# First loads of a fused attention and feed-forward kernel: x0 in two column halves on two DMA queues, V weights in two contraction halves, x1 between them, x1 statistics in quarters

## Chip, cores, metric

One core of one Trainium2 chip. The metric is the device time of one execution in microseconds, median of several runs. A profiled execution also gives a span, about 1.7 us shorter than its time.

## The reference, cut to what matters

```python
# S = 2048 rows, D = 1024, 32 heads of 32, window 256, F = 3584, all bf16
h  = x + attention(layernorm(x) @ wqkv) @ wo        # causal, sliding window of 256
h2 = h + silu(layernorm(h) @ w1) @ w2
# layernorm: (x - mean) / sqrt(var + 1e-5), over the 1024 columns of a row
```

The change concerns only the first 10 us: the layer norm of the first two tiles of 128 rows (x0, x1), their transposes, and the first product with the V part of `wqkv`.

## The kernel before

The first loads, in the order in which they are issued (`queue` is SyncE's unless named):

```python
def load_x(b, j, queue=nc.sync):
    queue.dma_start(out=x_ring[(b % 2) * 4 + j], in_=x2d[(b * 4 + j) * P:(b * 4 + j + 1) * P, :])

nc.scalar.activation(out=dummy[:], in_=eps[:], func=ACT.Sqrt)   # loads ScalarE's table
load_x(0, 0)                  # x0, 256 KB
load_wqkv(2 * D)              # first V weights, 8 contraction tiles, 1 MB
load_x(0, 1, nc.scalar)       # x1, on ScalarE's queue
load_x(0, 2)
load_wqkv(2 * D + 512)        # second V weights
load_x(0, 3)
load_wqkv(0)
# cut: identity, constants
for i in range(11):           # warm-up of TensorE's clock
    nc.tensor.matmul(o_ps[i % 2][:]..., lhsT=warm[:, 0, 0:P], rhs=warm[:, 0, :], start=True, stop=True)
```

Layer norm of x0 and x1, in the order of VectorE's instructions:

```python
def ln_half(xt, stats, c):
    nc.vector.bn_stats(out=stats[:, c, :], in_=xt[:, c * 512:(c + 1) * 512])

def ln_first(xt, st, rs, j, half_done=None, ahead=None):
    ln_stats(xt, st, j, half_done)                 # one or two ln_half, then bn_aggr
    nc.scalar.activation(out=rs[:, j:j + 1], in_=st[:, j, 1:2], func=ACT.Sqrt, bias=eps[:], scale=1.0)
    if ahead is not None:
        ln_half(ahead[0], ahead[1], 0)             # x1's first half while ScalarE takes the root
    nc.vector.reciprocal(out=rs[:, j:j + 1], in_=rs[:, j:j + 1])
    for h in range(4):
        ln_norm(xt[:, h * 256:(h + 1) * 256], st, rs, j)   # in place, a quarter at a time

ln_first(x_ring[0], st, rs, 0, None, (x_ring[1], half))
turn_first(x_ring[0], lnT_b[0], 0)     # 8 transposes on TensorE, 4 copies on ScalarE
ln_first(x_ring[1], st, rs, 1, half)
v_group(0, 0, 0, act, turn_1)          # 7 matmuls of x0, transposes of x1, eighth matmul
ln_first(x_ring[2], st, rs, 2)
v_group(0, 1, 0, act)                  # from here on TensorE has work without a break
```

The softmax here doesn't subtract the row's maximum and nothing guards it: scores larger than these inputs give would overflow.

## Time and profile before

| | before |
|---|---|
| median of the first 3 runs | 697.09 us (696.58 to 697.35) |
| span of the profiled execution | 695.5 us (its time 697.29) |
| TensorE busy | 99% of the span |
| TensorE's clock granted at full | from 5.30 us on |
| x0 landed / first statistic starts | 4.31 / 4.33 us |
| x1's normalization starts | 9.05 us |
| dense stretch (17 matmuls in a row) starts | 10.34 us |

A timeline line has the start, the time from the first to the last of the merged instructions, engine, line of the program, operation, output and inputs, how many, and in brackets how long the engine had been idle and for what. The last row is the one to keep in view. After it TensorE does not rest until the end, so a shift there should be a shift of the whole time.

### The profile page before, as it was taken

To read this page: it belongs to the slowest core of one execution; us is meant where nothing else is said; L and a number is where in the kernel's file an instruction comes from. 1 tells how busy PE (TensorE), PEld (TensorE's weight loads), DVE (VectorE), ACT (ScalarE), POOL (GpSimd) and SP (SyncE) were. 2 spreads that over 40 slices of the span, in tenths; PEclk is the share of its full clock that TensorE was granted. 3 is DMA by queue.
4 is the path that set the end of the run, shared out by engine and by line. 5 is a ranking of instruction groups with operands and counts; after the bars stand their busy time and mean duration, and the time that the engine had idled before them with its cause. 6 is when DMAs were issued, how large, how long until landed. Compare 5 with 4: busy or idle time off the path is not lost.

```text
span 695.5 us, 12334 instructions
## 1 busy us (share of the span) xinstructions
PE 690.1 (99%) x5091; PEld 331.6 (48%) x5091; DVE 289.5 (42%) x616; ACT 257.9 (37%) x328; POOL 174.5 (25%) x391
## 2 busy tenths in 40 slices
PE   8999999999999999999999999999999999999998
PEld 3444444555555555544444444444444444444445
DVE  6267646644443448544316134433133251244111
ACT  4326657777777777621310023300033100233000
POOL 1007667777777777500000000000000000000000
PEclk9999999999999999999999999999999999999999
DMA  7732131026231778880123410024200023100110
GB/s 241 257 53 77 35 93 51 17 60 193 70 124 23 205 251 272 199 311 31 31 76 99 107 38 1 1 83 77 83 1 1 11 95 91 45 1 1 30 39 24
DMA packets 76457, 60.84 MB, mean 87 GB/s; under 512 B 50288, under 2 KB 60528, under 8 KB 76400
## 3 DMA queue, kind: packets, MB, share of 16 engines
q1 hardware_dynamic: 76256, 59.78, 29.9%
q8 instruction: 40, 0.66, 0.4%
q10 hardware_dynamic: 144, 0.26, 0.1%
q14 instruction: 17, 0.14, 0.1%
HBM read 39.85 MB, written 8.39 MB: 69 GB/s over the span
## 4 chain that ended last, share of the span: by engine, by line
PE 99%; DMA 1%; DVE 0%; issue 0%
PE hacc L563 19%; PE hacc L600 17%; PE acc L248 16%; PE acc L600 10%; PE acc L563 9%; PE acc L238 8%; PE acc L267 7%; PE o_ps L339 4%; PE sc L285 3%; PE hacc L267 1%; PE o_ps L354 1%; PE sc L313 1%; DMA r_o<-in_A_x_dram 1%; PE tp L216 0%; DVE ln_st L169 0%; DVE r_o L197 0%
## 5 line engine op out<-in xcount | busy, mean ns | idle before, releaser
L330 POOL TENSOR_SCALAR_AFFINE_SELECT r_e<-r_e 128x256 bf16<-128x256 bf16 (+1 forms) x384 | 171.6, 477 | 116.5 <-ACT r_e L322 65.1
L293 ACT ACTIVATE r_e<-sc 128x1024 bf16<-128x1024 f32 x144 | 139.5, 1021 | 45.1 <-PE sc L285 31.0
L600 PEld LDWEIGHTS <-r_a 128*128 128x128 bf16 x952 | 90.9, 98 | 103.0
L563 PEld LDWEIGHTS <-r_w 128*128 128x128 bf16 x896 | 87.4, 98 | 104.8
L600 PE MATMUL hacc<-r_a 128*128 128x512 bf16 (+2 forms) x616 | 122.5, 360 | 0.0
L563 PE MATMUL hacc<-r_e,r_w 128*128 128x512 bf16 x456 | 100.9, 379 | 0.0
L572 ACT ACTIVATE r_n<-hacc 128x512 f32<-128x512 f32 x30 | 17.9, 597 | 178.9 <-PE hacc L563 178.9
L600 PE MATMUL acc<-r_a 128*128 128x512 bf16 x336 | 74.0, 379 | 0.0
L248 PEld LDWEIGHTS <-r_w 128*128 128x128 bf16 x512 | 46.5, 97 | 57.1 <-issue 7.0
L250 DVE CAST r_a<-acc 128x512 bf16<-128x512 f32 x56 | 38.7, 691 | 72.9 <-PE acc L248 56.3
L248 PE MATMUL acc<-r_t,r_w 128*128 128x512 bf16 x256 | 60.0, 379 | 0.0
L248 PE MATMUL acc<-r_w 128*128 128x512 bf16 x256 | 58.2, 380 | 0.0
L267 PE MATMUL acc<-r_o,r_a 128*128 128x512 bf16 x208 | 49.4, 380 | 0.0
L563 PE MATMUL acc<-r_e,r_w 128*128 128x512 bf16 x216 | 49.1, 379 | 0.0
L339 PEld LDWEIGHTS <-r_e 128*128 128x128 bf16 x1152 | 39.5, 96 | 17.0
L322 ACT ACTIVATE r_e<-sc 128x1024 bf16<-128x1024 f32 x36 | 34.9, 1021 | 21.2 <-PE sc L313 20.1
L339 PE MATMUL o_ps<-r_a,r_e 128*128 128x33 bf16 x1152 | 40.2, 178 | 0.0
L615 DVE SCALAR_TENSOR_TENSOR r_t<-hacc,r_t 128x512 bf16<-128x512 f32 (+2 forms) x22 | 14.0, 635 | 56.7 <-PE hacc L600 56.7
L267 PEld LDWEIGHTS <-r_a 128*128 128x128 bf16 x256 | 23.1, 98 | 29.6 <-issue 5.1
L615 DVE SCALAR_TENSOR_TENSOR r_t<-acc,r_t 128x512 bf16<-128x512 f32 x12 | 8.3, 692 | 64.2 <-PE acc L600 64.2
L573 DVE SCALAR_TENSOR_TENSOR r_a<-r_n,hacc 128x512 bf16<-128x512 f32 x30 | 20.6, 688 | 33.0 <-ACT r_n L572 33.0
L563 PE MATMUL hacc<-r_a,r_w 128*128 128x512 bf16 x144 | 32.9, 379 | 0.0
(71 smaller groups left out, 476.5 us busy)
## 6 DMA issues: line engine op xcount, KB each, us to landing
r_w<-in_B_w_dram SPq DMA_DIRECT2D x8, 896.0 KB, 5.1
r_a<-in_B_w_dram SPq DMA_DIRECT2D x7, 1024.0 KB, 7.9
r_w<-in_A_wqkv_dram SPq DMA_DIRECT2D x6, 1024.0 KB, 8.7
h_dram<-r_t SPq DMA_DIRECT2D x16, 256.0 KB, 3.0
r_t<-h_dram SPq DMA_DIRECT2D x16, 256.0 KB, 2.8
out_dram<-r_t SPq DMA_DIRECT2D x31, 128.0 KB, 1.7
r_o<-in_A_x_dram SPq DMA_DIRECT2D x15, 256.0 KB, 4.0
r_e<-h_dram SPq DMA_DIRECT2D x3, 1024.0 KB, 5.7
```

The costliest lines, as they stand in the source:

```text
L238: nc.tensor.matmul(acc, lhsT=lnT_b[b % 2][:, kt, j * P:(j + 1) * P], rhs=wv[:, kt, c * 512:(c + 1) * 512], start=(kt == 0), stop=(kt == KT ...
L248: nc.tensor.matmul(acc, lhsT=wqk[:, kt, col0:col0 + P], rhs=lnT_b[b % 2][:, kt, :], start=(kt == 0), stop=(kt == KT - 1))
L250: copy(out=(qT, kT)[which][b][:, g, :], in_=acc)
L267: nc.tensor.matmul(acc, lhsT=qT[b][:, g, j * P:(j + 1) * P], rhs=wo[:, g, c * 512:(c + 1) * 512], start=(g == 0), stop=(g == G - 1))
L285: nc.tensor.matmul(sc[hh // 2][:, hh % 2, ch * P:(ch + nq) * P], lhsT=kT[t // 4][r0:r0 + DH, g, (t % 4) * P:(t % 4 + 1) * P], rhs=qT[b][r0 ...
L293: nc.scalar.activation(out=e, in_=sc[pair], func=ACT.Exp, scale=scale)
L322: nc.scalar.activation(out=e, in_=sc[pair], func=ACT.Exp, scale=scale)
L330: nc.gpsimd.affine_select(out=ap, in_=ap, pattern=[[0, 2], [0, n], [sgn, P]], compare_op=ALU.is_ge if upper else ALU.is_gt, fill=0.0, base ...
L339: nc.tensor.matmul(o_ps[pair][:, qt * 2 + hh, 0:VW], lhsT=e_of(i, kind, pair)[:, hh, ch * P:(ch + 1) * P], rhs=v[:, b * 4 + kt, g * 4 + pa ...
L563: nc.tensor.matmul(acc, lhsT=w1[:, kt, ft * P:(ft + 1) * P], rhs=ln2T[b][:, kt, :], start=(kt == 0), stop=(kt == KT - 1))
L600: nc.tensor.matmul(acc[:, 0:c1 - c0], lhsT=gT[:, ft, j * P:(j + 1) * P], rhs=w2[ft // 4][:, ft % 4, c0:c1], start=(ft == 0), stop=(ft == F ...
L615: nc.vector.scalar_tensor_tensor(out=t_out[j % 2][:, c0:c1], in0=acc[:, 0:c1 - c0], scalar=0.5, in1=t_in[j % 2][:, c0:c1], op0=ALU.mult, o ...
```

## The change

The intent is to get the first matmuls under way sooner: x0 in two halves issued at the same moment from two engines, x1 next, V weights in two parts so that the first four contraction tiles can start on half of them, and a piece of x1's statistics small enough to fit into the wait for the square root.

```diff
-    nc.scalar.activation(out=dummy[:], in_=eps[:], func=ACT.Sqrt)
-    load_x(0, 0)
-    load_wqkv(2 * D)
-    load_x(0, 1, nc.scalar)
+    for queue, c0 in ((nc.sync, 0), (nc.scalar, 512)):
+        queue.dma_start(out=x_ring[0][:, c0:c0 + 512], in_=x2d[0:P, c0:c0 + 512])
+    load_x(0, 1)
+    for queue, k0 in ((nc.scalar, 0), (nc.sync, 4)):
+        queue.dma_start(out=wv[:, k0:k0 + 4, 0:512], in_=wqkv_v[:, k0:k0 + 4, 2 * D:2 * D + 512])
+    nc.scalar.activation(out=dummy[:], in_=eps[:], func=ACT.Sqrt)
...
+    def ln_quarter(xt, stats, c):
+        nc.vector.bn_stats(out=stats[:, c, :], in_=xt[:, c * 256:(c + 1) * 256])
...
-    ln_first(x_ring[0], st, rs, 0, None, (x_ring[1], half))
+    for c in range(2):
+        ln_half(x_ring[0], halves, c)
+    ln_first(x_ring[0], st, rs, 0, halves, lambda: ln_quarter(x_ring[1], quarters, 0))
     turn_first(x_ring[0], lnT_b[0], 0)
-    ln_first(x_ring[1], st, rs, 1, half)
+    for c in range(1, 4):
+        ln_quarter(x_ring[1], quarters, c)
+    ln_first(x_ring[1], st, rs, 1, quarters)
```

(`ln_first` now starts at the aggregate. x2 and x3 keep their old form.)

More of the change, by code (lines that the diff above doesn't have):

```diff
@@ L201, in ln_transpose, with ln_first, ln_whole @@
         nc.sync.dma_start_transpose(out=dst[:, :, j * P:(j + 1) * P], in_=xt)
-    def ln_first(xt, st, rs, j, half_done=None, ahead=None):
-        ln_stats(xt, st, j, half_done)
+    def ln_first(xt, st, rs, j, stats, ahead=None):
+        nc.vector.bn_aggr(out=st[:, j, :], in_=stats[:])
         nc.scalar.activation(out=rs[:, j:j + 1], in_=st[:, j, 1:2], func=ACT.Sqrt, bias=eps[:], scale=1.0)
         if ahead is not None:
-            ln_half(ahead[0], ahead[1], 0)
+            ahead()
+        nc.vector.reciprocal(out=rs[:, j:j + 1], in_=rs[:, j:j + 1])
+        for h in range(4):
+            ln_norm(xt[:, h * 256:(h + 1) * 256], st, rs, j)
+    def ln_quarter(xt, stats, c):
+        nc.vector.bn_stats(out=stats[:, c, :], in_=xt[:, c * 256:(c + 1) * 256])
+    def ln_whole(xt, st, rs, j):
+        ln_stats(xt, st, j)
+        nc.scalar.activation(out=rs[:, j:j + 1], in_=st[:, j, 1:2], func=ACT.Sqrt, bias=eps[:], scale=1.0)
         nc.vector.reciprocal(out=rs[:, j:j + 1], in_=rs[:, j:j + 1])
@@ L387 @@
     st, rs = ln_tiles("a")
-    half = small.tile([P, 2, 6], F32, name="ln_st", tag="ln_st")
-    ln_first(x_ring[0], st, rs, 0, None, (x_ring[1], half))
+    halves = small.tile([P, 2, 6], F32, name="ln_st", tag="ln_st")
+    quarters = small.tile([P, 4, 6], F32, name="ln_st1", tag="ln_st1")
+    for c in range(2):
+        ln_half(x_ring[0], halves, c)
+    ln_first(x_ring[0], st, rs, 0, halves, lambda: ln_quarter(x_ring[1], quarters, 0))
     turn_first(x_ring[0], lnT_b[0], 0)
-    ln_first(x_ring[1], st, rs, 1, half)
+    for c in range(1, 4):
+        ln_quarter(x_ring[1], quarters, c)
+    ln_first(x_ring[1], st, rs, 1, quarters)
     def turn_1(kt):
@@ L397 @@
     v_group(0, 0, 0, act, turn_1)
-    ln_first(x_ring[2], st, rs, 2)
+    ln_whole(x_ring[2], st, rs, 2)
     v_group(0, 1, 0, act)
-    ln_first(x_ring[3], st, rs, 3)
+    ln_whole(x_ring[3], st, rs, 3)
     ln_transpose(x_ring[3], lnT_b[0], 3)
```

## The prediction

> **What bounds the kernel now.** I read the page first. It gives TensorE 99% of the span, and in its forty slices only the first and the last are not full:
>
> ```profile
> PE   8999999999999999999999999999999999999998
> ```
>
> The busy times by stretch say it more sharply: from 10.34 to 690 us TensorE is busy in 679.65 of 679.66 us. So the change, which touches only the first microseconds, can win or lose only what it does to the moment at which this unbroken stretch begins. The view of waits, for TensorE alone, has two entries:
>
> ```profile
> PE o_ps L165 <- DVE r_e L160: 1.6, 1, 1.6
> PE tp L216 <- DVE r_o L197: 1.0, 1, 1.0
> ```
>
> The first is ahead of the warm-up matmuls and stays. The second is the wait for the first normalized x tile. Next I read the chain of waits, cut to the first 40 us:
>
> ```profile
> 0.81 3.51 DMA r_o<-in_A_x_dram
> ...
> 4.33 1.30 DVE ln_st L169 x2
> ...
> 5.66 0.21 DVE st_a L177
> 5.87 0.56 DVE ln_st L169
> ...
> 6.52 0.36 DVE r_o L197
> ...
> 6.93 1.06 PE tp L216 x8
> 7.98 1.51 PE acc L238 x7
> 9.49 1.01 PE tp L216 x8
> 10.51 3.67 PE acc L238 x17
> ```
>
> The reader should see: x0 lands at 4.31; two statistics, an aggregate, then 0.56 us in which the chain runs through a statistic that belongs to x1, not x0; then the normalization and the transposes. From 6.93 on the chain calls TensorE the bound, but this hides a second one, seen in the timeline:
>
> ```profile
> 5.78 0.64 DVE L169 BATCH_NORM_STATS2 ln_st<-r_o 128x6 f32<-128x512 bf16 x1
> 6.34 0.15 DVE L208 RECIPROCAL rs_a<-rs_a 128x1 f32<-128x1 f32 x1
> 6.52 1.12 DVE L197 TENSOR_SCALAR r_o<-r_o,st_a,rs_a 128x256 bf16<-128x256 bf16 x4
> 7.55 0.69 DVE L169 BATCH_NORM_STATS2 ln_st<-r_o 128x6 f32<-128x512 bf16 x1
> 8.28 0.21 DVE L177 BATCH_NORM_AGGREGATE st_a<-ln_st 128x2 f32<-128x12 f32 x1
> 9.05 1.12 DVE L197 TENSOR_SCALAR r_o<-r_o,st_a,rs_a 128x256 bf16<-128x256 bf16 x4
> 9.45 1.05 PE L216 MATMUL tp<-ident,r_o 128*128 128x128 bf16 x8
> 10.34 3.83 PE L238 MATMUL acc<-r_w 128*128 128x512 bf16 x17
> ```
>
> VectorE hardly rests from 4.33 to 8.5. The second set of eight transposes (x1) begins 0.40 us after x1's normalization begins, and takes 1.05 us; the same eight at about 14.0, where the data is ready, take 0.61. They are paced by VectorE. So the dense stretch begins when **x1** is normalized, at the end of one serial VectorE chain: x0 landing, x0 statistics, x0 normalization, x1 statistics, x1 normalization. That is where I read the worth of the change.
>
> How the loads share the engines is in the DMA view of two short windows, 2.2 to 2.6 and 3.2 to 3.4 us (packets, MB, share). q1 is SyncE's queue, q10 is ScalarE's, on which x1 was issued at 0.97:
>
> ```profile
> q1 hardware_dynamic: 39, 0.08, 82.4%
> ...
> q10 hardware_dynamic: 28, 0.06, 101.8%
> q1 hardware_dynamic: 4, 0.00, 1.1%
> ```
>
> x1 did not share with x0: each engine drained x0 and then x1, and began the V weights after that. The packet records give x0's 2048-byte packets from 1.82, 84 ns each and 80 apart, eight to an engine, after a first packet of 0.1 to 0.88 us; fourteen of the sixteen engines were through x0 by 3.29. Two sat 0.92 and 0.98 us on one packet and ended at 3.86 and 3.93; 0.38 us after that x0 counted as landed. Stalls of this kind come at random (packets of x1 show 0.37 to 0.65). Landings, issue plus time to landing: x1 4.87, the first V weights 1.26 + 6.3 = 7.56, x2 8.32.
>
> **What the Trainium skill says.** "DMA: Bandwidth & Descriptors", section "Issuing engines are not separate DMA queues": queues of different engines run on the same 16 DMA engines and interleave, and a second one saves only issue time. The windows above agree: one queue followed the other at full share, no bandwidth was added. Its section "Queues, rings and completion order" says that an engine goes round robin between queue rows a packet at a time; here the turn passed after a whole tile. "VectorE: DVE Perf Modes", "The TRN2 errata", says that short operations pay a fixed cost for each instruction; two 512-column statistics end 1.29 us after the first starts, one takes 0.68, so they start 0.61 apart, against 0.53 for 512 elements at that page's 0.96 GHz. "TensorE: Matmul & The Clock Gate", Part 1, says that some 3.4 us of activity lift the clock; the warm-up matmuls start 0.43 us apart until about 5, and it is not touched.
>
> **The change part by part.**
>
> (a) x0 as two halves. No byte is removed. Two transfers of 128 KB replace one of 256; ScalarE can issue at about 0.81 instead of 0.97, since its table load moves behind. What is new is that statistics of the first half need only the first half. Eight packets of 1024 bytes take 8 x 42 ns (their start-to-start later in this trace) = 0.34 us an engine, half of x0's 0.67. Without late stalls the first half is through by about 2.95 to 3.0 and lands near 3.4, the second by 3.3, landing near 3.7. Then the second statistic ends at 3.4 + 1.29 = 4.7, against 5.62 now: 0.9 to 1.0 won. With a stall as long as that of the trace on the second half alone (4.31), it ends at 4.31 + 0.68 = 4.99: 0.63 won. With the stall on the first half too (3.95), 5.24: 0.38 won. I take **0.65**.
>
> (b) The piece of x1 done while ScalarE takes the square root is a quarter. Now the reciprocal begins 0.68 after the aggregate does (6.34 - 5.66); where nothing sits between, for x2, 0.57 (11.96 - 11.39). A quarter, estimated at 0.27 + 0.08 = 0.35 plus 0.07 of latency, begins 0.12 after the aggregate and ends at 0.54: it fits. Won: **0.11**.
>
> (c) The rest of x1's statistics is three quarters instead of a half: 3 x 0.35 = 1.05 against 0.61, on the VectorE chain: lost **0.44**. Half of it is moved work, half the fixed cost.
>
> (d) V weights in two halves. The first four of eight contraction tiles can start when 0.5 MB have landed. Now the weights land at 7.56 and the first matmul starts at 7.82, held by the copy that ended at 7.64. If x0's path moves 0.76 earlier, its first matmul could start near 7.06, and the undivided 7.56 would have become a wait of 0.5; at 42 ns a packet and 32 packets to an engine the first half lands about 1.3 us before the whole, near 6.2 to 6.5. So (d) wins nothing by itself, it keeps a wait from appearing. Even with it in the old form the seven matmuls (1.5 us) would still end by 9.1, about when x1's transposes become ready.
>
> Sum for the start of the dense stretch: -0.65 - 0.11 + 0.44 = **-0.32 us**. Everything later keeps its order: x2 landed at 8.32 and is wanted at 10.08 - 0.3; the second V weights landed 2.34 + 8.7 = 11.04 and are wanted near 12.3 - 0.3; x3 11.63 against 13.20 - 0.3. So 697.09 - 0.32 = 696.77; I say 696.7.
>
> **Rivals.** One: *the second quarter waits for x1.* x1 now follows the first half on SyncE's queue, and 512 KB of weights follow the second half on ScalarE's. If each engine takes them in the order halves, x1, weights, x1 lands about where it did (4.87), against a need at 5.78 - 0.65 = 5.13. If the weights get in first, 32 packets of 42 ns put x1 back by 1.35 us, to about 6; the quarter would hold VectorE, in order, ahead of x0's reciprocal at 6.4, (a) and (b) would be gone and (c) stays: 697.4 to 697.5. For it: the two issuing engines start within 0.02 us of each other (ScalarE's first work 0.80, SyncE's 0.81). Against: ScalarE's weights carry 512 rows to x1's 128, and in this trace each engine finished small tiles before the weights. I give it one in four.
>
> Two: *the late stalls are the landing time.* Then halving the transfer changes nothing for the slower half, (a) is 0.3 and the sum is zero: 697.1. The old kernel's own three runs spread 0.77 us, about one such stall.
>
> Three: *all of (a)*, no stall: -0.97 - 0.11 + 0.44 = -0.64, 696.4. The floor below that is the warm-up, whose last matmul starts at 5.44 and has issued by 5.65, with the transposes then ready at 5.9.
>
> **Range and chances.** Rivals two and three with run-to-run spread of 0.3 to 0.4 either way give 695.9 to 697.5 for 8 in 10. 2% would be 14 us, more than the whole stretch before 10.34; so within 2% is all but certain: 0.99, the rest split.
>
> **What would show it.** x0's first statistic starts before 4.0 in place of 4.33, and the second follows it at once or waits for the other half; the reciprocal follows the aggregate by 0.57; three quarters take about 1.1 us; x1's transposes begin near 9.1 in place of 9.45; the long stretch of 17 matmuls begins near 10.0 in place of 10.34; the rest is unchanged to a tenth. It is wrong if VectorE shows a wait for the x tensor ahead of the quarter statistic, if TensorE waits for weights (a gap between kt 3 and 4 of the first group, or ahead of kt 0), or if the start of the dense stretch moves and the time does not.

## The result, and the profile after

| | before | after |
|---|---|---|
| median of 6 runs | 696.99 us (696.58 to 697.35) | 697.16 us (696.98 to 698.8) |
| ratio | | 1.0007, 95% interval 0.9994 to 1.002 |
| span of the profiled execution (its time) | 695.5 (697.29) | 695.2 (696.99) |
| x0's first statistic | 4.33 | 3.50 |
| x1's normalization | 9.05 | 8.56 |
| dense stretch | 10.34 | 9.85 |

A ratio is the mean time of one kernel's runs over the mean of the other's of the same rounds, so it is not quite the ratio of the medians.

The two lines of numbers contradict each other. The two traces say 0.3 us faster, the runs say 0.17 us slower or level. The chain of waits of the changed kernel, cut to its first 40 us (start, duration, what):

```profile
0.80 2.68 DMA r_o<-in_A_x_dram
...
3.50 1.30 DVE ln_st L171 x2
...
5.07 0.30 ACT rs_a L208
...
5.60 1.12 DVE r_o L199 x4
6.71 1.00 DVE ln_st L216 x3
...
8.03 0.30 ACT rs_a L208
...
8.56 0.35 DVE r_o L199
...
8.96 1.05 PE tp L229 x8
10.02 3.67 PE acc L251 x17
```

The chain now shows openly what had to be argued from the timeline of the kernel before: from 3.50 to 8.91 it is VectorE's, with ScalarE's two square roots, and TensorE enters only at x1's transposes. The statistic of x1 is gone from the wait for the first root. The three quarters of x1 are in it. The chain counts the dense stretch only from the end of the transposes; the timeline has its first matmul:

```profile
9.85 3.83 PE L251 MATMUL acc<-r_w 128*128 128x512 bf16 x17
```

Matmul by matmul, the shift between the two traces is -0.49 us at the start of the dense stretch and -0.41 at the last of the 5091 matmuls. It changes in one place only, at 19.6 us, by 0.08. This is the wait that goes with it, from the view of waits in the first 25 us (who, for what: us in total, times, longest):

```profile
PEld L251 <- DMA r_w<-r_o: 0.4, 1, 0.4
PE tp L229 <- DVE r_o L199: 0.4, 1, 0.4
```

The first line is the weight load for x3's first product. It waits for x3's transpose by DMA, which landed 3.2 us after issue here and 2.8 before. Weight loads run ahead of the matmuls, so of 0.4 us only 0.08 was lost. The second line is a wait that the kernel before did not have: x1's transposes, at 8.96, wait for x1's normalization. The 1.0 us for which x0's transposes waited before is gone. The tail (last matmul to end of span) took 3.17 us instead of 3.07. So in these two executions a gain of 0.49 us at 10 us arrives at the end as 0.31.

The DMA view of the window from 2.4 to 2.8 us (queue: packets, MB, share) shows what became of the two halves:

```profile
q1 hardware_dynamic: 63, 0.06, 47.2%
q10 hardware_dynamic: 62, 0.06, 45.9%
```

SyncE's queue (q1, left half) and ScalarE's (q10, right half) are served in equal numbers. The completion writes of the left half came between 2.83 and 3.12 us, those of the right between 2.92 and 3.21, so the left half was in only 0.09 us ahead of the right one. The packet records do not name the DMA engine. That each engine alternates packet by packet is inferred from the equal numbers and from this even shift.

What remained to be explained: why the runs do not show the 0.3 us that the traces show.

### The profile page after: what moved, and what is told of

Same layout as the page of the kernel before. It is cut to its first block, busy times and chain, and to the rows that moved or that the text cites. A ratio compares the mean times of both kernels' runs of the same rounds, so it can differ in the third digit from the quotient of the medians.

```text
span 695.2 us, 12339 instructions
## 1 busy us (share of the span) xinstructions
PE 690.3 (99%) x5091; PEld 331.7 (48%) x5091; DVE 289.9 (42%) x618; ACT 257.9 (37%) x328; POOL 174.6 (25%) x391
## 4 chain that ended last, share of the span: by engine, by line
PE 98%; DVE 1%; DMA 0%; ACT 0%; issue 0%
PE hacc L581 19%; PE hacc L618 17%; PE acc L261 16%; PE acc L618 10%; PE acc L581 9%; PE acc L251 8%; PE acc L280 7%; PE o_ps L352 4%; PE sc L298 3%; PE hacc L280 1%; PE o_ps L367 1%; PE sc L326 1%; DMA r_o<-in_A_x_dram 0%; PE tp L229 0%; DVE r_o L199 0%; DVE ln_st L171 0%
```

## The experiments

Kernels are compared only within the same rounds. Three readings went in. **S**: the first trace of the kernel before was an execution with a late x0. Against a usual one nothing is won, and the quarters cost. **G**: the gain is in every run and the runs are only noisy. **I**: what is issued together on two queues is interleaved, and this delays x1. The intervals of this timing are about 0.12% (0.8 us) either way, so the time alone settles little here. The traces settle more.

### before_2: the kernel before, a second trace

No edit.

> The kernel before, unchanged, for a second trace. Theory S (the first trace of the kernel before fell on an execution whose x0 landed late, at 4.31, because two DMA engines sat on one packet; a usual execution has x0 in by 3.7 to 3.9): x0's first statistic starts at 3.7 to 3.9, the 17 matmuls of the dense stretch at 9.7 to 9.9, the span is 694.8 to 695.1, and the runs of this kernel spread by some 0.6 us. Theory G (4.31 is usual, and the gain of 0.3 us that the two traces show is there in every run): statistic at 4.2 to 4.4, dense stretch at 10.3, span 695.5.

Measured: 696.4 us (5 runs, 696.28 to 697.86), the kernel before in the same rounds 696.64 (9 runs). Span 694.6. Timeline of this execution:

```profile
3.46 1.28 DVE L169 BATCH_NORM_STATS2 ln_st<-r_o 128x6 f32<-128x512 bf16 x2 [1.96 <-DMA r_o<-in_A_x_dram]
...
7.29 1.67 PE L238 MATMUL acc<-r_w 128*128 128x512 bf16 x7 [0.20 <-DMA r_w<-in_A_wqkv_dram]
...
9.46 3.83 PE L238 MATMUL acc<-r_w 128*128 128x512 bf16 x17
```

The same kernel, with x0's statistics 0.87 us earlier than in its first trace, and as early as the changed kernel's. The packet records say why: no packet of x0 took over 0.33 us here, where two had taken 0.92 and 0.98. The dense stretch starts at 9.46, earlier even than S expected (9.7 to 9.9). S holds, and G falls. The middle line is of use too: with x0 early, the undivided V weights do become a wait, of 0.20 us, and it moves nothing. The dense stretch starts 6.00 us after the first statistic, as it does without the wait (10.34 - 4.33 = 6.01).

### after_2 and after_3: the changed kernel, two more traces

No edit.

> The changed kernel, unchanged, for a second trace. Both theories: x0's first statistic at 3.4 to 3.6, three quarters in 1.07 us, dense stretch at 9.8 to 9.9, span 695.2 with little spread, except where the clock of TensorE rises late. Theory S: equal to the kernel before or 0.1 to 0.3 us slower in the same rounds. Theory G: 0.3 us faster.

> The changed kernel, unchanged, for a third trace. Theory (its loads are even, its statistics cost 0.34 us more, and x1 comes late in some executions because the first half of V is served descriptor by descriptor beside it): x0's first statistic 3.4 to 3.7; dense stretch 6.35 us after it if x1 is there at 4.9, up to 6.9 if VectorE waits for x1; 0.3 to 0.7 us above the kernel before of the same rounds. Rival (the two traces above were chance): as fast as the kernel before.

Measured: after_2 697.51 us (696.76 to 697.74), kernel before 696.64 in the same rounds; after_3 697.47 (696.85 to 699.5), kernel before 696.73. Ratios 1.0009 (0.9996 to 1.0021) and 1.0013 (1.0001 to 1.0025). Timeline of after_2:

```profile
3.56 1.29 DVE L171 BATCH_NORM_STATS2 ln_st<-r_o 128x6 f32<-128x512 bf16 x2 [2.06 <-DMA r_o<-in_A_x_dram]
...
5.62 0.43 DVE L216 BATCH_NORM_STATS2 ln_st<-r_o 128x6 f32<-128x256 bf16 x1 [0.54 <-DMA r_o<-in_A_x_dram]
...
10.40 3.83 PE L251 MATMUL acc<-r_w 128*128 128x512 bf16 x17
```

My expectation for after_2 had no wait for x1, and it was wrong: VectorE waits 0.54 us for it, in order, ahead of x0's reciprocal, and the dense stretch begins 6.84 us after the first statistic instead of 6.35. after_3 has the same wait with 0.31 us (dense stretch at 10.35). x1 landed at 4.5 in the first trace of the changed kernel and at 5.6 in these two. In after_2, from 4.0 to 4.4 us, the DMA view has

```profile
q1 hardware_dynamic: 27, 0.06, 56.7%
q10 hardware_dynamic: 31, 0.03, 22.6%
```

where q1 carries x1 (2 KB packets) and q10 the first half of V (1 KB): the weights go in between x1's packets. This is the prediction's first rival, in two of three traces.

### quarters_only and x1_halves: the statistics by themselves

quarters_only is the kernel before with the one edit

```diff
-            ln_half(ahead[0], ahead[1], 0)        # ahead of the reciprocal
+            ln_quarter(ahead[0], ahead[1], 0)
...
+            for c in range(1, 4):                 # after x0's normalization
+                ln_quarter(xt, half_done, c)
```

and x1_halves is the changed kernel with that part undone:

```diff
-    ln_first(x_ring[0], st, rs, 0, halves, lambda: ln_quarter(x_ring[1], quarters, 0))
+    ln_first(x_ring[0], st, rs, 0, halves, lambda: ln_half(x_ring[1], quarters, 0))
-    for c in range(1, 4):
-        ln_quarter(x_ring[1], quarters, c)
+    ln_half(x_ring[1], quarters, 1)
```

> The kernel before with x1's statistics in quarters, loads untouched. If the quarters cost 0.32 net: from x0's first statistic to the start of the dense stretch 6.01 us (10.34 - 4.33) become 6.3 to 6.35, and the time is 0.3 us above the kernel before of the same rounds. Rival: no change, 6.0 us.

> The changed kernel with x1's statistics in halves again (one in the wait for the square root, one after x0's normalization), all loads as changed. If quarters cost what they seem to (1.07 + 0.26 us against 0.69 + 0.21, less 0.11 won at the reciprocal): reciprocal 0.68 after the aggregate starts instead of 0.58, x1's normalization 0.3 us earlier, dense stretch at 9.5 to 9.6, span 694.9, some 0.3 us under the changed kernel. Rival: the quarters cost nothing because x1's transposes wait for something else (copies on ScalarE, V weights): dense stretch at 9.85 as before.

Measured: quarters_only 697.09 us (697.02 to 697.28), kernel before 696.64. Timeline:

```profile
3.94 1.29 DVE L169 BATCH_NORM_STATS2 ln_st<-r_o 128x6 f32<-128x512 bf16 x2 [2.44 <-DMA r_o<-in_A_x_dram]
...
7.06 1.07 DVE L204 BATCH_NORM_STATS2 ln_st<-r_o 128x6 f32<-128x256 bf16 x3
...
10.29 3.83 PE L246 MATMUL acc<-r_w 128*128 128x512 bf16 x17
```

From first statistic to dense stretch: 6.35 us, against 6.01 and 6.00 in the kernel before. The timeline of x1_halves:

```profile
3.46 1.29 DVE L171 BATCH_NORM_STATS2 ln_st<-r_o 128x6 f32<-128x512 bf16 x2 [1.96 <-DMA r_o<-in_A_x_dram]
...
9.50 3.92 PE L251 MATMUL acc<-r_w 128*128 128x512 bf16 x17
```

This is 9.50 - 3.46 = 6.04, against 6.35 in the changed kernel (9.85 - 3.50). Both directions agree on 0.31 to 0.35 us for the quarters. Its times do not follow so cleanly: 697.22 us, from 696.56 (the profiled run) to 698.27. The loads are still those of the change, and the runs that were not profiled have no trace. That they had a late x1 is likely but not shown.

### x0_split_only and x0_split_2: the split of x0 by itself, twice

```diff
-    load_x(0, 0)
+    for queue, c0 in ((nc.sync, 0), (nc.scalar, 512)):
+        queue.dma_start(out=x_ring[0][:, c0:c0 + 512], in_=x2d[0:P, c0:c0 + 512])
     # the table load of ScalarE, then as before: V whole on SyncE's queue, x1 on ScalarE's
```

> The kernel before with only x0's load split: left half on SyncE's queue, right half on ScalarE's, x1 behind it on ScalarE's queue, V weights whole on SyncE's, statistics in halves. Theory I (two queues issued together are served descriptor by descriptor, so both halves finish at the time the whole tile would, and what stands behind the halves on both queues is interleaved too): x0's first statistic at 3.4 to 3.6, second right after the first, no gain over an unstalled execution of the kernel before (3.46); x1 (2 KB packets) shares with weights (1 KB) and lands at 4.6 to 5.2 against 4.17 to 4.87 there. Rival (the prediction's step a): the left half lands 0.3 us ahead of the right and the statistic starts at 3.1 to 3.2.

> The kernel with only x0's load split, again, to see whether its 0.25 us under the kernel before holds: x0's first statistic 3.4 to 3.7, dense stretch 6.0 us later, time 0.1 to 0.3 us under the kernel before of the same rounds, narrow spread. Rival: level with it, within 0.1 us.

Measured: the same kernel gave 696.63 us (696.59 to 697.09, kernel before 696.88) and 699.1 us (696.58 to 700.12, kernel before 696.73), which I had not expected. In the second its six runs fall into two groups: 696.58 and 696.79, and four from 699.01 to 700.12. The first trace has x0's first statistic at 3.68, no wait for x1, dense stretch at 9.68 (6.00 later). The second trace is of the other group. One line of its timeline, one of its stretches (window, length, busy us of TensorE with count, weight loads, VectorE, ScalarE, GpSimd, granted clock, DMA share, GB/s), and the queues from 3.2 to 3.6 us:

```profile
6.94 0.69 DVE L170 BATCH_NORM_STATS2 ln_st<-r_o 128x6 f32<-128x512 bf16 x1 [1.97 <-DMA r_o<-in_A_x_dram]
```

```profile
7.83:11.24 3.41, 3.11 (x14) 1.36 (x15) 2.98 (x11) 1.46 (x5) 0.00 (x0) 0.50 1.08 389
```

```profile
q1 hardware_dynamic: 130, 0.13, 102.1%
```

x1, issued at 1.31, landed at 6.9: V's packets, issued at 1.26 on the other queue, went first and then between. VectorE stood 1.97 us ahead of x0's reciprocal. TensorE, left without work from 5.5 to 8.1, fell back to half its clock from 7.83 to 11.24. Part 1 of the Trainium skill's "TensorE: Matmul & The Clock Gate" gives 3413 ns for the window after which the clock changes, and the 3.41 us here agree. The first group's seven matmuls took 2.75 us instead of 1.67, and the dense stretch began at 12.11, which is 8.67 us after the first statistic.

So the split of x0 gains little by itself, and moving x1's issue to the same moment as the weights makes its landing a lottery. In the kernel before, x1 was issued at 0.97 and the weights at 1.26, 0.29 us later. In this kernel x1 came 0.03 and 0.05 us after them, in the changed one 0.03 us after. That this distance decides is an inference, and no run changed it alone. It is not all: the same 0.03 us gave landings at 4.5 and at 5.6 in the changed kernel.

Over all traces, x0's first statistic: whole x0, six traces, 3.46 to 4.33, mean 3.80; split x0, eight traces, 3.44 to 4.03, mean 3.62. The standard error of the difference of 0.18, worked out from these fourteen numbers, is 0.15, so it can't be told from none.

### v_split_only: the split of V by itself

```diff
-    load_wqkv(2 * D)
     load_x(0, 1, nc.scalar)
+    for queue, k0 in ((nc.scalar, 0), (nc.sync, 4)):
+        queue.dma_start(out=wv[:, k0:k0 + 4, 0:512], in_=wqkv_v[:, k0:k0 + 4, 2 * D:2 * D + 512])
```

> The kernel before with only the first V weights split in halves of the contraction: ScalarE's queue carries x1 and then the first half, SyncE's x0 and then the second. Theory: the halves do not move the dense stretch; x0's first statistic between 3.4 and 4.3 as luck has it, start of the dense stretch 6.0 us later, first matmul of the first group without a wait for weights. The time is that of the kernel before within 0.2 us. Rival: weights of the second half get between x0 and x1 on the engines, x1 is later and VectorE waits for it: 0.2 to 0.6 us slower.

Measured: 697.54 us (697.43 to 697.68), kernel before 696.88. VectorE does not wait for x1, so neither the theory nor the rival was right. TensorE waits for weights:

```profile
8.35 1.67 PE L239 MATMUL acc<-r_w 128*128 128x512 bf16 x7 [0.86 <-ACT rs_a L206]
```

The bracket names ScalarE's square root, whose result this matmul does not use. The matmul's own semaphore is that of the weights, issued on ScalarE's queue at 1.40 and landed 6.9 us later, at 8.3. The half that is wanted first stood behind x1, with the other half interleaved, and was complete later than the whole weights are in the kernel before (7.2 to 7.6). Here the wait reaches the dense stretch: it begins at 10.30, 6.46 after the first statistic, since x1's transposes come after the seven matmuls in TensorE's order.

### one_queue: everything on SyncE's queue

```diff
-    load_wqkv(2 * D)
-    load_x(0, 1, nc.scalar)
+    load_x(0, 1)
+    load_wqkv(2 * D)
```

> The kernel before with x0, x1 and the whole V weights on SyncE's queue in this order, nothing on ScalarE's. Theory I: nothing interleaves with x0 or x1, so x1 lands at 4.2 to 4.6 in nearly every execution and VectorE never waits for it; x0's first statistic 3.4 to 3.9; V weights 0.3 to 0.5 us later, TensorE waits for them up to 0.6 us ahead of the first group, but the dense stretch still begins 6.0 us after x0's first statistic; the time equals the kernel before or is 0.1 to 0.3 us less. Rival: the later weights move the dense stretch by 0.3 us or more.

Measured: 699.57 us (697.18 to 701.93, 6 runs), kernel before 696.88, ratio 1.0036 (1.0018 to 1.0054). In the profiled run, the fastest, the start is as theory I has it: first statistic 3.75, no wait for x1, 0.53 us wait for V, dense stretch 6.13 us later. But this trace loses another 0.41 us against before_2, at 167 and 249 us. At the first of these places the timeline shows ScalarE's exponential waiting for a buffer that GpSimd still had to mask. Why the start should matter there stays open. For the other runs, up to 4.7 us longer, the record has part of the reason: the four from 699.30 to 701.93 us have a mean granted clock of 0.998 or 0.995, the two near 697.2 one of 1.000. An estimate from x0_split_2's trace: one stretch of 3.41 us at half clock lowers the mean over 697 us by 0.0024 and costs at most 1.7 us, so 0.998 is about one such stretch and 0.995 about two. When in these runs the clock fell has no trace.

### pool_norm: GpSimd takes part of the normalization

A try at a faster version: loads on one queue with V in two halves, and

```diff
+            pool = h >= {0: 2, 1: 3}.get(j, 4)
-            ln_norm(xt[:, h * 256:(h + 1) * 256], st, rs, j)
+            ln_norm(xt[:, h * 256:(h + 1) * 256], st, rs, j, nc.gpsimd if pool else nc.vector)
```

> A try at a version that beats both: loads on one queue with V in two halves, statistics in halves, and GpSimd normalizes the last two quarters of x0 and the last quarter of x1 beside VectorE. If the VectorE chain is the bound (x1's normalization starts it): x0's share on VectorE 0.52 us shorter, x1's last quarter some 0.3 us earlier, dense stretch 5.3 to 5.5 us after x0's first statistic instead of 6.0, time 0.5 to 0.7 us under the kernel before. If GpSimd takes over 0.6 us for a quarter, or the two engines hold each other up: no gain, or slower.

Measured: 698.27 us (698.19 to 699.46), kernel before 696.88. The instructions of that line (durations in ns, least/median/most):

```profile
L198 POOL TENSOR_SCALAR r_o<-r_o,st_a,rs_a x3: 1218/1291/1292, 5.7 to 9.5; 128x256 bf16<-128x256 bf16 x3
```

1.29 us for what VectorE does in 0.34. The dense stretch began 7.47 us after the first statistic. A failure, by the condition written ahead of it.

### x1_ahead and x1_paired: x1 out of the way of the weights

Both start from x1_halves. x1_ahead puts both halves of V on SyncE's queue, behind x1:

```diff
-    for queue, k0 in ((nc.scalar, 0), (nc.sync, 4)):
+    for queue, k0 in ((nc.sync, 0), (nc.sync, 4)):
```

x1_paired splits x1 like x0, so that the two queues carry the same:

```diff
-    load_x(0, 1)
+    for queue, c0 in ((nc.sync, 0), (nc.scalar, 512)):
+        queue.dma_start(out=x_ring[1][:, c0:c0 + 512], in_=x2d[P:2 * P, c0:c0 + 512])
```

> The changed kernel with x1's statistics in halves and both halves of V on SyncE's queue behind x1, so that ScalarE's queue carries only the right half of x0. If the V weights beside x1 are what delays it: x1's last completion write before 4.3 us in place of 4.18 to 5.18, no wait of VectorE for x1, dense stretch 6.0 us after x0's first statistic (3.5), 9.5; and the time 0.1 to 0.3 us under the kernel before. If x1's delay is chance of the same size in any order, x1 is again seen at 4.5 to 5.2 and the time spreads as for x1_halves.

> The changed kernel with statistics in halves and x1 in two column halves too, on both queues behind those of x0, then the two halves of V. Theory: the two queues are served in pairs, so x1 is complete before either half of V moves: last completion write of x1 near 4.2, no wait for it; both halves of V finish together, about 7.0 to 7.5, and TensorE waits up to 0.6 us for them without moving the dense stretch, which starts 6.0 us after x0's first statistic. Time as x1_ahead. Rival: more and smaller transfers finish later, 0.2 us or more above.

Measured: x1_ahead 698.18 us (697.45 to 698.74), x1_paired 701.56 (698.05 to 702.35), kernel before 696.73. Of the mechanism the first half is right. In both traces VectorE has no wait for x1, which landed at 4.7 and at 4.4. But both are slower than the kernel before, by more than the changed kernel is, against my expectation. TensorE in x1_ahead:

```profile
8.78 0.81 PE L251 MATMUL acc<-r_w 128*128 128x512 bf16 x3 [0.24 <-DMA r_w<-in_A_wqkv_dram]
...
12.47 1.90 PE L251 MATMUL acc<-r_w 128*128 128x512 bf16 x8 [0.33 <-DMA r_w<-in_A_wqkv_dram]
```

The dense stretch begins 6.00 us after the first statistic (4.03, a late one), and is then broken at 12.47 by the second V weights, issued at 3.30 instead of 2.34 because SyncE has more to issue before. This costs a further 0.49 us. In x1_paired TensorE waits 1.67 us for V, until 8.89, and the dense stretch begins 7.27 us after the first statistic. The profiled run is the fastest of its six. The other five have no trace, but all have a mean clock of 0.998 or 0.995, against 1.000 here: again TensorE at half clock for a part of each. The runs of x1_ahead have a full clock, and what took them to 698.74 stays open.

No version beat the kernel before.

## Why the prediction was right or wrong

The time, 697.16, lies in the range of 695.9 to 697.5 and within 2%, but 0.46 above the point, and the gain of 0.3 us did not come. The three medians lie above the kernel before, though only the third interval (1.0001 to 1.0025) leaves out no change. That the time fell into the range is in part luck: two errors in different steps, no gain from (a) and now and then a late x1, are both small beside the width of the range. By its steps:

- **The bound** (the dense stretch begins when x1 is normalized, at the end of one serial VectorE chain) held. In the first after trace, in before_2 and in quarters_only the stretch begins 1.29 to 1.30 us after x1's normalization, as before (10.34 - 9.05), and a shift there arrived at the last matmul up to 0.08 us. Over all traces, span less start of the dense stretch is 685.1 to 685.4 us in eleven of fourteen, and 685.6 to 685.7 in one_queue, pool_norm and x1_ahead. The exceptions are the runs where V came late (v_split_only, x1_paired, a little one_queue), where TensorE's own order took over, x0_split_2 with its half clock, and pool_norm, where GpSimd set the pace.
- **(a), x0 in halves: -0.65. This is the step that failed**, twice over. It took 4.31 as the usual landing, from one trace. A second trace of the same kernel had 3.43 (statistic at 3.46). And it let the left half land 0.3 us ahead of the right, while the two queues were served in equal numbers (63 and 62 packets in 0.4 us) and the left half was 0.09 us ahead. Over all traces the split is worth 3.80 - 3.62 = 0.18 us, give or take 0.15, with executions of the one kernel 0.87 us apart. The prediction's second rival ("the late stalls are the landing time") comes nearest to this. It still put (a) at 0.3 and the sum at zero.
- **(b), the quarter in the root's wait: -0.11.** Reciprocal 5.40 - 4.82 = 0.58 after the aggregate, where 0.57 was forecast and 0.68 measured before: 0.10. Right, where x1 is there. The quarter's cost was an estimate from a page's clock (0.27 + 0.08). The starts measured here, 0.61 us apart for 512 columns and 0.35 for 256, give 0.26 for the columns and 0.09 fixed.
- **(c), three quarters after: +0.44.** x0's normalization to x1's is 8.56 - 5.60 = 2.96 us, before 9.05 - 6.52 = 2.53: +0.43. Right in size, but not "half of it moved work, half the fixed cost": by these figures it is 0.26 for the moved quarter and 0.17 for two more instructions. (b) and (c) together: +0.33, and 0.31 to 0.35 by experiment.
- **(d), V in halves: no gain, keeps off a wait.** In the changed kernel there is no wait for weights. In before_2 the wait avoided was 0.20 us, where 0.5 was forecast, and moved nothing. Right in kind. The same split in another order of queues cost 0.46 us.
- **Rival one, x1 late behind weights**, given one chance in four, came in two of three traces: the reciprocal follows the aggregate by 1.09 and 0.86 us instead of 0.58, so +0.51 and +0.28. Its size was predicted larger and its mechanism as one block ahead. It was interleaving.

(Rival three's floor has a misreading that changes nothing here: 5.44 is the end of the last warm-up's weight load, its matmul starts at 5.56.)

With the sizes as measured: -0.18 - 0.10 + 0.43 + 0.26 (mean of 0, 0.51 and 0.28) = +0.41 us. The mean start of the dense stretch was 10.20 in three traces of the changed kernel and 9.90 in two of the kernel before, +0.30; the medians differ by 0.17, 0.87 and 0.74 us in three sets of rounds. The runs at 698.8 and 699.5 are likely such as x0_split_2's trace shows: both have a mean clock of 0.998, and neither has a trace. The record bears this out as a pattern. Of the 69 runs of the changed kernel and of the experiments, all 16 with a mean clock of 0.998 or less took 698.80 us or more, and the other 53 at most 698.74. In the 36 runs of the kernel before with a clock on record (before_2 included) it never was under 0.999. So new loads can cost more than the wait itself, by way of the clock. The prediction had no such term.

## What to carry to other kernels

A wait for a first load is a draw from a spread, so take two or three traces of the kernel before, before a gain is worked out against one of them. Splitting a transfer over two queues did not bring its first half clearly sooner here, and what is issued within some hundredths of a microsecond on the two queues may be interleaved or swapped; the data wanted next seems safer issued clearly earlier than issued beside (an inference, see x0_split_2). Look at the clock of every run, also of those without a trace. Cutting an operation to fit a gap pays only if the rest of it, with its fixed costs, does not return to the same chain.

## What the Trainium skill lacked or had wrong

- "DMA: Bandwidth & Descriptors", section "Queues, rings and completion order": turns go round by packets of some 9 to 17 descriptors. A packet in the views here is a single row, and 128 rows on 16 engines are 8 for each. That x1 followed x0 as a whole in the kernel before, issued 0.16 us later on the other queue, agrees with such a turn. That the two halves of x0 shared evenly (63 and 62 packets in 0.4 us, their completion writes 0.09 us apart) does not. Nothing tells which of the two happens: the same kernel had x1 landed at 4.8 in one execution and at 6.9 us in another.
- The same page, section "Issuing engines are not separate DMA queues", is right that a second queue adds no bandwidth: the two halves together took 47.2% and 45.9% of the engines. It lacks what order to expect of two queues issued within 0.05 us, and that this can differ between executions. A wide spread of times is not owed to a second queue alone: one_queue, all on one, ran from 697.18 to 701.93 us.
- The same page has no figure for how single packets of a first load stall: 0.92 and 0.98 us here, where 84 ns is usual. One such packet among 128 can set the landing time of the tile.
- "GPSIMD Engine Reference", section "Engine selection": operations with one tensor input are roughly at line rate. A normalization of 128x256 bf16 with two operands of one value per partition took 1.29 us on GpSimd against 0.34 on VectorE. With this one size, a fixed cost and a rate can't be told apart.
- No page has a duration for the batch-norm statistics: 0.68 us for 512 columns, 0.37 for 256, starts 0.61 and 0.35 us apart.
